# Token rows for the expert blocks: two gathers of whole rows and a way through memory to quarter rows, in place of eight gathers of quarter rows

## The chip, the cores and the metric

The kernel runs on one core of a Trainium2 chip. A core has a matrix engine (TensorE, PE in the profile), a vector engine (VectorE, DVE), a scalar engine (ScalarE, ACT), GpSimd (POOL) and SyncE (SP). On this kernel SyncE does nothing but start plain transfers, and GpSimd starts all transfers whose addresses come from a list (gathers and scatters). The metric is the device time of one execution in microseconds (us); it is shown as the median of several runs, and one more execution is taken with a profiler.

## The reference

Attention over pooled keys and values, then a mixture of experts in which each token goes to one expert. Tokens whose local gate is at or above one half take over the expert of the token before.

```python
k_p = k.reshape(B, H, Sp, 8, D).mean(axis=3); v_p = v.reshape(B, H, Sp, 8, D).mean(axis=3)
scores = scale * np.matmul(q, k_p.transpose(0, 1, 3, 2))
attn_out = softmax(scores) @ v_p                       # B=8, H=8, S=576, D=64
x = attn_out.transpose(0, 2, 1, 3).reshape(B, S, 512)  # 4608 tokens of 512 numbers
logits = np.einsum('bsd,de->bse', x, w_gate)           # 8 experts
for b in range(B):
    prev_e = -1
    for s in range(S):
        fresh_e = int(np.argmax(logits[b, s]))
        e = fresh_e if s == 0 or local_gate[b, s] < 0.5 else (prev_e if prev_e >= 0 else fresh_e)
        prev_e = e
        p = softmax(logits[b, s])
        h = np.maximum(x[b, s] @ w1[e], 0.0)           # 512 -> 1024
        out[b, s] = p[e] * (h @ w2[e])                 # 1024 -> 512
```

## The kernel before, in words

**Two stages.** The first 230 us or so are attention: units of 128 queries, in an order written out by hand (`PLAN`). Each unit's token rows are written to a table in memory, `x_rows`, one row of 512 numbers for each token. For each token a router ranks it within its expert and scatters the token's number and its gate value into lists in memory (`ids`). The second stage, from about 250 us to the end, is the experts: blocks of 256 tokens of one expert each. The first of them stand in hand-written lists (`PLAN_B`, `PLAN_C`; one word is one step, `M1` and `M2` being the two products of block 0), then come `block 1` and a chain of blocks 2, 3, ... under branches (`blocks`), until the tokens run out.

**One block.** Weights are held as a high and a low part, so each product is three products. `l1_two` makes eight groups of hidden columns; `l1_mms` writes group f to one of the buffers `hp` (three of them in block 1, six later), and `l1_h` (ACT copy L338, DVE add L339) and `l1_l` (L343, L344) take it out. `l2(1)` and `l2(0)` (L352) make the two halves of the output rows, `emit_scale` (DVE, L1061) scales a half into `ob`, and `emit_rows` (POOL, L1064) scatters its 128 rows to `out`. Where a block has 128 tokens or fewer, `single` is used in place of `l1_two`.

**How a block's tokens get in.** `ids_load(b+4)` (SP, four transfers into `idp`, L300) reads a piece of the lists. `ids_sum` (DVE, L304, L305) turns it into row numbers of quarter rows, `idk`; `meta` (L308 to L311) picks the token numbers `mi` and gate values `ms` that the output needs. `gather` (POOL, L315) then starts eight gathers, each of 128 quarter rows (512 bytes each), into `xk`, whose partition 32a+s holds quarter a of the tokens s, 32+s, 64+s and so on. With this layout one DVE instruction in `x_turn` (L319) transposes all 32x32 pieces at once, and `x_split` (L324, L325) makes the two parts that TensorE reads. `ahead(b)` does lists, `meta` and `gather` for block b+3, after `l1_two(b)`; the rows are transposed in `x_turn` at the start of block b+2. So `xk` has two buffers. For blocks 2 and 3 these steps are the words `f1` to `f4` of `PLAN_B`, and `x_turn(2)` stands in front of `l1_two(1)`.

**What sets the order.** Each engine runs its own instructions in program order. Two transfers that write the same tensor are ordered by the framework: the second is started when the first has landed. The two scatters of a block both write `out`, so they follow each other in this way. The weights of the next expert are loaded by SP (L207, L211) into `raw1` and `raw2` and split by ACT and DVE (L214, L215, L219, L220) when the expert changes.

Of the kernel before, what the change touches and what calls it, by code (L numbers as in the profile page):

```python
# [16 lines left out]
P = 128  # L17
B, H, S, HD = 8, 8, 576, 64
POOL = 8
# [77 lines left out]
M1:0 M1:1 M1:2 M1:3 i2:0 M1:4 M1:5 f0:0 f1:0 i3:0 f2:0 M1:6 M1:7 YR:0 M2:0 M2:1 M2:2 M2:3 Y1:0 M2:4 M2:5 Y0:0 f3:0 i4:0 f4:0 M2:6 M2:7  # L97
""")
PLAN_C = plan("""
ld:0 M2:8 M2:9 M2:10 M2:11 e1:0 M2:12 M2:13 M2:14 M2:15  # L100
# [3 lines left out]
def moe_attention(ctx: ExitStack, tc: tile.TileContext, q, q_st, k, v, w_gate, w_local, w1, w2, out):  # L104
# [60 lines left out]
    picked = const.tile([P, 2, 2, 5], F32, name="picked")  # L165
    nc.vector.memset(picked, 0.0)
    nc.vector.tensor_scalar(out=picked[:, :, 0, 4], in0=quad.broadcast_to([P, 2]), scalar1=-0.25, scalar2=None, op0=ALU.mult)
# [76 lines left out]
    idp = route.tile([P, 5, TB, 2], F32, name="idp", bufs=1)  # L244
    ids4 = route.tile([P, TB, 2], F32, name="ids4", bufs=1)
    idk = [route.tile([P, TB], I32, name=f"idk{i}", bufs=1) for i in range(2)]
    nc.gpsimd.memset(idp[:, 4], 0.0)
    nc.gpsimd.tensor_copy(out=idp[:, 4, :, 0], in_=quad.broadcast_to([P, TB]))
    x_pc = x_rows.rearrange("n (a d) -> (n a) d", d=PC)
# [53 lines left out]
    def ids_sum(b):  # L303
        nc.vector.tensor_reduce(out=ids4, in_=idp.rearrange("p u j w -> p j w u"), axis=AX.X, op=ALU.add)  # L304
        nc.vector.tensor_copy(out=idk[b % 2], in_=ids4[:, :, 0])  # L305

    def meta(b):
        nc.vector.tensor_tensor(out=picked.rearrange("p h w j -> p h j w")[:, :, 0:4, :],  # L308
# [4 lines left out]
    def gather(b):  # L313
        for j in range(TB):
            nc.gpsimd.indirect_dma_start(out=xk[b % 2][:, j, :], out_offset=None, in_=x_pc,  # L315
                                         in_offset=bass.IndirectOffsetOnAxis(ap=idk[b % 2][:, j:j + 1], axis=0))
# [39 lines left out]
    with ExitStack() as actx:  # L356
# [399 lines left out]
        xk, xtb, xr_t, sp = {}, {}, None, None  # L756
        xgs, xts, xtp = {}, {}, {}

        def do(name, n):
# [144 lines left out]
            elif op == "f1":  # L904
                ids_sum(2)
                meta(2)
            elif op == "f2":
                xk.update({i: ld.tile([P, TB, PC], F32, name="kt", bufs=2) for i in range(2)})
                xr_t = ld.tile([P, KD, 2 * P], F32, name="qt", bufs=4)
                gather(2)  # L910
            elif op == "f3":
                ids_sum(3)
                meta(3)
            elif op == "f4":
                gather(3)
            elif op == "i4":
# [186 lines left out]
    def ahead(b):  # L1103
        ids_sum(b + 3)
        meta(b + 3)
        gather(b + 3)
        ids_load(bass.ds(entry(b + 4, 1, (EN.SP,), NU32 - TB), TB))
# [12 lines left out]
    def rest(b, two):  # L1120
# [10 lines left out]
        emit_rows(b, 1)  # L1131
        l2(0)
# [64 lines left out]
```

## Time and profile before

| what | value |
|---|---|
| median of 3 runs | 695.61 us (692.05 to 696.6) |
| the profiled execution | 693.06 us, span 691.4 us from its first to its last instruction |
| PE busy over the span | 621.9 us (90%) |
| DVE, ACT, POOL busy | 448.8, 272.4, 381.9 us |
| the eight gathers a block (L315) | 176 instructions, 180.7 us busy on POOL, mean 1027 ns |
| moved by transfers started on POOL | 22.60 MB, 10.3% of 16 engines' span |
| moved by transfers started on SP | 74.38 MB, 32.1% |

Busy shares are averages over both stages. An engine's share tells how much it does, not whether anyone waits for it; that is read in a stretch, from the idle time in front of instructions and from what ended it. A time is an instruction's start after the first instruction of the span. A transfer's instruction ends when it has been handed over, not when the data has arrived; the time to landing stands in a view of its own.

### The profile page before, as it was taken

To read this page: it belongs to the slowest core of one execution; us is meant where nothing else is said; L and a number is where in the kernel's file an instruction comes from. 1 tells how busy PE (TensorE), PEld (TensorE's weight loads), DVE (VectorE), ACT (ScalarE), POOL (GpSimd) and SP (SyncE) were. 2 spreads that over 40 slices of the span, in tenths; PEclk is the share of its full clock that TensorE was granted. 3 is DMA by queue.
4 is the path that set the end of the run, shared out by engine and by line. 5 is a ranking of instruction groups with operands and counts; after the bars stand their busy time and mean duration, and the time that the engine had idled before them with its cause. 6 is when DMAs were issued, how large, how long until landed. Compare 5 with 4: busy or idle time off the path is not lost. (4 is left out here: it accounts for less than half of the span.)

```text
span 691.4 us, 11897 instructions
## 1 busy us (share of the span) xinstructions
PE 621.9 (90%) x3588; PEld 526.4 (76%) x3588; DVE 448.8 (65%) x1026; ACT 272.4 (39%) x612; POOL 381.9 (55%) x431
## 2 busy tenths in 40 slices
PE   2878799789698899999999999999999999999990
PEld 1767688678577788878888878788887887888880
DVE  5567589997966764636548647678945478854440
ACT  1134345355454333313326326366613267432230
POOL 5256566876757455565454455474655535555432
PEclk7579799997779899999999999999999999999996
DMA  7988784645431212821114521718722118722111
GB/s 207 298 284 277 258 265 141 195 145 170 128 131 63 77 34 75 297 73 48 55 56 138 192 69 41 294 52 283 271 81 65 42 55 288 274 67 65 40 48 35
DMA packets 50230, 98.10 MB, mean 142 GB/s; under 512 B 23630, under 2 KB 23634, under 8 KB 50132
## 3 DMA queue, kind: packets, MB, share of 16 engines
q1 hardware_dynamic: 39348, 74.38, 32.1%
q0 software_dynamic: 10784, 22.60, 10.3%
q8 instruction: 39, 0.64, 0.4%
q14 instruction: 59, 0.48, 0.2%
HBM read 76.84 MB, written 22.21 MB: 143 GB/s over the span
## 5 line engine op out<-in xcount | busy, mean ns | idle before, releaser
L315 POOL DMA_INDIRECT kt<-x_rows,idk x176 | 180.7, 1027 | 113.8 <-DVE picked L308 64.7
L331 PE MATMUL hp<-x,w1h 128*128 128x512 f32 x376 | 135.9, 402 | 0.1
L352 PE MATMUL o_ps<-w2h,ht_h 128*128 128x512 f32 x312 | 122.8, 394 | 1.5 <-PEq L1128 0.9
L352 PE MATMUL o_ps<-w2h,ht_l 128*128 128x512 f32 x312 | 122.0, 391 | 0.0
L352 PE MATMUL o_ps<-w2l,ht_h 128*128 128x512 f32 x312 | 121.6, 390 | 0.0
L333 PE MATMUL hp<-x,w1l 128*128 128x256 f32 x376 | 106.2, 282 | 0.0
L338 ACT COPY hs<-hp 128x256 f32<-128x256 f32 x94 | 34.8, 370 | 147.4 <-PE hp L333 146.9
L331 PEld LDWEIGHTS hp<-x,w1h 128*128 128x128 f32 x376 | 71.3, 190 | 17.9 <-DVE hs L339 0.6
L567 PE MATMUL op<-vaug,aT 128*128 128x148 f32 (+4 forms) x448 | 77.9, 340 | 2.1 <-ACT aT L377 1.8
L567 PEld LDWEIGHTS op<-vaug,aT 128*128 128x128 f32 (+1 forms) x448 | 69.4, 202 | 8.8 <-ACT aT L377 3.1
L333 PEld LDWEIGHTS hp<-x,w1l 128*128 128x128 f32 x376 | 71.7, 191 | 0.9 <-DVE w1l L215 0.3
L352 PEld LDWEIGHTS o_ps<-w2h,ht_h 128*128 128x128 f32 x312 | 58.6, 188 | 14.6 <-ACT ht_h L961 2.5
L352 PEld LDWEIGHTS o_ps<-w2h,ht_l 128*128 128x128 f32 x312 | 58.5, 188 | 13.5 <-DVE ht_l L962 0.7
L343 ACT ACTIVATE ht_h<-hs 128x256 fp32r<-128x256 f32 x136 | 57.2, 421 | 29.1 <-DVE hs L339 29.1
L352 PEld LDWEIGHTS o_ps<-w2l,ht_h 128*128 128x128 f32 x312 | 58.6, 188 | 11.5
L344 DVE SCALAR_TENSOR_TENSOR ht_l<-hs,ht_h 128x256 fp32r<-128x256 f32 x136 | 59.1, 435 | 5.9 <-ACT ht_h L343 5.6
L339 DVE TENSOR_TENSOR hs<-hp,hs 128x256 f32<-128x256 f32 x94 | 38.7, 415 | 31.3 <-ACT hs L338 30.8
L1061 DVE TENSOR_SCALAR ob<-o_ps,ms 128x512 f32<-128x512 f32 x22 | 16.5, 748 | 51.7 <-PE o_ps L352 50.3
L1064 POOL DMA_INDIRECT out<-ob,mi x22 | 23.0, 1047 | 46.1 <-DVE mi L311 10.8
L383 POOL TENSOR_TENSOR t<-vt_in 128x512 f32<-128x512 f32 (+1 forms) x22 | 25.1, 1140 | 39.1 <-DMA vt_in<-in_v 38.7
L703 POOL DMA_INDIRECT ids<-pm,pos x36 | 35.7, 991 | 19.3 <-DVE pos L700 9.4
L377 ACT COPY osb<-op 128x444 f32<-128x444 f32 (+2 forms) x56 | 26.5, 476 | 47.8 <-PE op L567 43.2
(250 smaller groups left out, 1135.9 us busy)
## 6 DMA issues: line engine op xcount, KB each, us to landing
raw<-in_moe_w SPq DMA_DIRECT2D x56, 512.0 KB
kk<-in_k SPq DMA_DIRECT2D x16, 576.0 KB
vt_in<-in_v SPq DMA_DIRECT2D x16, 512.0 KB
qt<-in_q SPq DMA_DIRECT2D x16, 512.0 KB
x_rows<-xs SPq DMA_DIRECT2D x16, 512.0 KB
kt<-x_rows,idk POOLq DMA_INDIRECT x176, 2.6
vt_in<-in_v SPq DMA_DIRECT2D x8, 256.0 KB
vt_in<-in_moe_w SPq DMA_DIRECT2D x4, 512.0 KB
```

The costliest lines, as they stand in the source:

```text
L315: nc.gpsimd.indirect_dma_start(out=xk[b % 2][:, j, :], out_offset=None, in_=x_pc, in_offset=bass.IndirectOffsetOnAxis(ap=idk[b % 2][:, j:j ...
L331: nc.tensor.matmul(out=ps, lhsT=W1[0][:, kk, f * P:(f + 1) * P], rhs=xt[:, kk].rearrange("p i n -> p (i n)"), start=(kk == 0), stop=False, ...
L333: nc.tensor.matmul(out=ps[:, 0:2 * P], lhsT=W1[1][:, kk, f * P:(f + 1) * P], rhs=xt[:, kk, 0, :], start=False, stop=(kk == KD - 1), skip_g ...
L338: nc.scalar.copy(out=hb[:, 0, :], in_=ps[:, 2 * P:])
L339: nc.vector.tensor_tensor(out=hb[:, 1, :], in0=ps[:, 0:2 * P], in1=hb[:, 0, :], op=ALU.add)
L343: nc.scalar.activation(out=ht[0][:, f, :], in_=hb, func=AF.Relu)
L344: nc.vector.scalar_tensor_tensor(out=ht[1][:, f, :], in0=hb, scalar=0.0, in1=ht[0][:, f, :].bitcast(F32), op0=ALU.max, op1=ALU.subtract)
L352: nc.tensor.matmul(out=to[h], lhsT=ht[i][:, kk, h * P:(h + 1) * P], rhs=W2[j][:, kk, :], start=(n == 0), stop=(n == 3 * KF - 1))
L377: nc.scalar.copy(out=out, in_=in_)
L383: nc.gpsimd.tensor_tensor(out=t4[:n, 0:m], in0=src[:, :, 0:256], in1=src[:, :, 256:512], op=ALU.add)
L567: nc.tensor.matmul(out=out, lhsT=lhs, rhs=rhs if len(out.shape) == 3 else rhs.rearrange("p s x -> p (s x)"), start=all(x[0] != n for x in ...
L703: nc.gpsimd.indirect_dma_start(out=ids[u % 4].rearrange("t m w -> (t m) w"), out_offset=bass.IndirectOffsetOnAxis(ap=pos[:, u:u + 1], axis=0),
```

## The change

The eight gathers of quarter rows become two gathers of 128 whole rows each (2 KB a row) into `xg`, with the token numbers `mi` as row numbers. A new function `quarters` brings them into the layout that `xk` had: SP writes the 256 rows to a scratch table `xd` in memory (two of them, in turn), and then reads them back with four transfers, one for each quarter a, into partitions 32a to 32a+31. `quarters(b+3)` stands in `rest`, after the first scatter of block b and in front of `l2(0)`; for blocks 2 and 3 it stands in the plans as `qr:2` (after `f4`) and `qr:3` (in front of `ld`, the first load of `raw1` and `raw2`). `ids_sum` goes: `idk` and its cast are no longer needed, and the fifth column of `idp`, which added the number of the quarter, goes with it. `xg` uses two buffers of the pool where attention kept keys (`kk`).

```diff
--- before.py
+++ after.py
@@ -94,10 +94,10 @@
 XR:1 L1:4 rR:3 ct:0 rV:3 rP:3 h0:4 h1:4 s:0 s:0 s:0 s:0 s:0 s:0 s:0 s:0 s:0 L1:5 tc:0 cn:0 i1:0 h0:5 h1:5
 tb:0 tb:1 L1:6 h0:6 h1:6 tb:2 tb:3 L1:7 h0:7 h1:7 tb:4 tb:5 tb:6 tb:7 L2:0 L2:1 L2:2 X1:1 L2:3 X1c:1 L2:4
 X0:1 L2:5 X0c:1 L2:6 L2:7 es:1 L2:8 L2:9 so:1 L2:10 L2:11 g1:0 L2:12 L2:13 L2:14 L2:15 es:0 so:0
-M1:0 M1:1 M1:2 M1:3 i2:0 M1:4 M1:5 f0:0 f1:0 i3:0 f2:0 M1:6 M1:7 YR:0 M2:0 M2:1 M2:2 M2:3 Y1:0 M2:4 M2:5 Y0:0 f3:0 i4:0 f4:0 M2:6 M2:7
+M1:0 M1:1 M1:2 M1:3 i2:0 M1:4 M1:5 f0:0 f1:0 i3:0 f2:0 M1:6 M1:7 YR:0 M2:0 M2:1 M2:2 M2:3 Y1:0 M2:4 M2:5 Y0:0 f3:0 i4:0 f4:0 qr:2 M2:6 M2:7
 """)
 PLAN_C = plan("""
-ld:0 M2:8 M2:9 M2:10 M2:11 e1:0 M2:12 M2:13 M2:14 M2:15
+qr:3 ld:0 M2:8 M2:9 M2:10 M2:11 e1:0 M2:12 M2:13 M2:14 M2:15
 """)
 
 @with_exitstack
@@ -162,9 +162,7 @@
     nc.vector.tensor_scalar(out=prow_i, in0=prow_i, scalar1=5, scalar2=None, op0=ALU.arith_shift_right)
     nc.vector.tensor_copy(out=quad, in_=prow_i)
     pickm = const.tile([P, 2, 4, 2], F32, name="pickm")
-    picked = const.tile([P, 2, 2, 5], F32, name="picked")
-    nc.vector.memset(picked, 0.0)
-    nc.vector.tensor_scalar(out=picked[:, :, 0, 4], in0=quad.broadcast_to([P, 2]), scalar1=-0.25, scalar2=None, op0=ALU.mult)
+    picked = const.tile([P, 2, 2, 4], F32, name="picked")
     for j in range(4):
         for w, f in ((0, 0.25), (1, 1.0)):
             nc.vector.tensor_scalar(out=pickm[:, :, j, w], in0=quad.broadcast_to([P, 2]), scalar1=float(j), scalar2=f,
@@ -241,12 +239,9 @@
     ps_r = ctx.enter_context(tc.tile_pool(name="ps_r", bufs=1, space=PSUM))
     ms = [route.tile([P, 2, 2], F32, name=f"ms{i}", bufs=1) for i in range(NM)]
     mi = [route.tile([P, 2], I32, name=f"mi{i}", bufs=1) for i in range(NM)]
-    idp = route.tile([P, 5, TB, 2], F32, name="idp", bufs=1)
+    idp = route.tile([P, 4, TB, 2], F32, name="idp", bufs=1)
     ids4 = route.tile([P, TB, 2], F32, name="ids4", bufs=1)
-    idk = [route.tile([P, TB], I32, name=f"idk{i}", bufs=1) for i in range(2)]
-    nc.gpsimd.memset(idp[:, 4], 0.0)
-    nc.gpsimd.tensor_copy(out=idp[:, 4, :, 0], in_=quad.broadcast_to([P, TB]))
-    x_pc = x_rows.rearrange("n (a d) -> (n a) d", d=PC)
+    xd = [dram.tile([2 * P, D], F32, name=f"xd{i}") for i in range(2)]
 
     idns = [route.tile([P, 4, 2, 2], F32, name=f"idn{i}", bufs=1) for i in range(NS + 1)]
     idms = [route.tile([P, 2, 2], F32, name=f"idm{i}", bufs=1) for i in range(NS + 1)]
@@ -300,20 +295,22 @@
             nc.sync.dma_start(idp[:, u].rearrange("p j w -> p (j w)"),
                               ids[u][:, r, :].rearrange("t j w -> t (j w)").unsqueeze(0).broadcast_to([4, 32, 2 * TB]))
 
-    def ids_sum(b):
+    def meta(b):
         nc.vector.tensor_reduce(out=ids4, in_=idp.rearrange("p u j w -> p j w u"), axis=AX.X, op=ALU.add)
-        nc.vector.tensor_copy(out=idk[b % 2], in_=ids4[:, :, 0])
-
-    def meta(b):
-        nc.vector.tensor_tensor(out=picked.rearrange("p h w j -> p h j w")[:, :, 0:4, :],
+        nc.vector.tensor_tensor(out=picked.rearrange("p h w j -> p h j w"),
                                 in0=ids4.rearrange("p (h j) w -> p h j w", h=2), in1=pickm, op=ALU.mult)
         nc.vector.tensor_reduce(out=ms[b % NM], in_=picked, axis=AX.X, op=ALU.add)
         nc.vector.tensor_copy(out=mi[b % NM], in_=ms[b % NM][:, :, 0])
 
     def gather(b):
-        for j in range(TB):
-            nc.gpsimd.indirect_dma_start(out=xk[b % 2][:, j, :], out_offset=None, in_=x_pc,
-                                         in_offset=bass.IndirectOffsetOnAxis(ap=idk[b % 2][:, j:j + 1], axis=0))
+        for h in range(2):
+            nc.gpsimd.indirect_dma_start(out=xg[b % 2][:, h, :], out_offset=None, in_=x_rows[0:NT + 1],
+                                         in_offset=bass.IndirectOffsetOnAxis(ap=mi[b % NM][:, h:h + 1], axis=0))
+
+    def quarters(b):
+        nc.sync.dma_start(xd[b % 2].rearrange("(h p) d -> p h d", h=2), xg[b % 2])
+        for a in range(4):
+            nc.sync.dma_start(xk[b % 2][32 * a:32 * a + 32], xd[b % 2][:, PC * a:PC * (a + 1)].rearrange("(j s) c -> s j c", s=32))
 
     def x_turn(b):
         nc.vector.transpose(out=xr_t.rearrange("p k (j t) -> p j k t", t=32),
@@ -753,7 +750,7 @@
         first1, first2, lgs = {}, {}, {}
         reg = {}
 
-        xk, xtb, xr_t, sp = {}, {}, None, None
+        xk, xg, xtb, xr_t, sp = {}, {}, {}, None, None
         xgs, xts, xtp = {}, {}, {}
 
         def do(name, n):
@@ -902,17 +899,19 @@
             elif op == "f0":
                 rows_meta(1, NS)
             elif op == "f1":
-                ids_sum(2)
                 meta(2)
             elif op == "f2":
                 xk.update({i: ld.tile([P, TB, PC], F32, name="kt", bufs=2) for i in range(2)})
+                xg.update({i: ld.tile([P, 2 * G * POOL], F32, name="kk", bufs=3)[:, 0:2 * D].rearrange("p (h d) -> p h d", h=2)
+                           for i in range(2)})
                 xr_t = ld.tile([P, KD, 2 * P], F32, name="qt", bufs=4)
                 gather(2)
             elif op == "f3":
-                ids_sum(3)
                 meta(3)
             elif op == "f4":
                 gather(3)
+            elif op == "qr":
+                quarters(n)
             elif op == "i4":
                 ids_load(bass.ds(entry(4, 1, (EN.SP,), NU32 - TB), TB))
             elif op == "i3":
@@ -1101,7 +1100,6 @@
         load2(rl2, nx)
 
     def ahead(b):
-        ids_sum(b + 3)
         meta(b + 3)
         gather(b + 3)
         ids_load(bass.ds(entry(b + 4, 1, (EN.SP,), NU32 - TB), TB))
@@ -1129,6 +1127,7 @@
                 l2(1)
         emit_scale(b, 1)
         emit_rows(b, 1)
+        quarters(b + 3)
         l2(0)
         with tc.If(chg > 0):
             weights2(nx)
```

**SyncE at the start of block 1.** The queue between the last list load (`i4`, the last of four `idp` transfers) and the first weight loads (`raw`). Before:

```order
L300 DMA idp<-ids_67 128x1x16 [waits DMAHW1_49]
L225 TENSOR_LOAD tab
L207 ISA
L207 DMA raw_3020<-in_moe_w 128x1024 [waits DMASW1_49,DMASW2_49,DMASW0_49,DMASW3_49,PE_49,Activation_49]
L207 ISA
L207 DMA raw_3020<-in_moe_w 128x1024
```

In the changed kernel (`kk` is the pool's name for `xg`, `kt` that for `xk`):

```order
L295 DMA idp<-ids_67 128x1x16 [waits DMAHW1_49]
L311 DMA xd_188<-kk 128x2x512 [waits DMASW5_49,DMASW4_49]
L313 DMA kt<-xd_188 32x8x128 [waits DMAHW6_49,Activation_49]
L313 DMA kt<-xd_188 32x8x128 x2
L313 DMA kt<-xd_188 32x8x128 [waits DMAHW2_49]
L311 DMA xd_189<-kk 128x2x512 [waits DMAHW3_49,DMASW7_49,DMASW6_49]
L313 DMA kt<-xd_189 32x8x128 [waits DMAHW4_49,DMAHW3_49,Activation_49]
L313 DMA kt<-xd_189 32x8x128 [waits DMAHW5_49]
L313 DMA kt<-xd_189 32x8x128
L313 DMA kt<-xd_189 32x8x128 [waits DMAHW7_49]
L223 TENSOR_LOAD tab
```

Ten transfers now stand between the list load and the first weight load: for block 2 and then for block 3 one write to `xd`, and four reads behind it that wait for that write.

**GpSimd in a block of the chain, from its gathers to its last scatter.** The words are the same in every block. Before:

```order
L315 DMA kt<-x_rows,idk_191 128x128 x8
L225 TENSOR_LOAD tab
L1123 COMPARE_AND_BRANCH
L1123 UNCONDITIONAL_BRANCH x2
L1128 UNCONDITIONAL_BRANCH
L1064 DMA out<-ob_2465,mi_184 4608x512
L1133 COMPARE_AND_BRANCH
L1133 UNCONDITIONAL_BRANCH x2
L1064 DMA out<-ob_2465,mi_184 4608x512
```

In the changed kernel:

```order
L307 DMA kk<-x_rows,mi_180 128x512 x2
L223 TENSOR_LOAD tab
L1121 COMPARE_AND_BRANCH
L1121 UNCONDITIONAL_BRANCH x2
L1126 UNCONDITIONAL_BRANCH
L1063 DMA out<-vt_in,mi_183 4608x512
L1132 COMPARE_AND_BRANCH
L1132 UNCONDITIONAL_BRANCH x2
L1063 DMA out<-vt_in,mi_183 4608x512
```

Two instructions stand in front of the two scatters where there were eight.

## Rows read from the trace of the kernel before

**Rows 1.** The head of the profile's page: the span, each engine's busy time with its share and its instructions, and the span in 40 slices of 17.3 us (busy tenths of PE and POOL, and the clock that TensorE was granted in tenths of 2.4 GHz).

```profile
span 691.4 us, 11897 instructions
...
PE 621.9 (90%) x3588; PEld 526.4 (76%) x3588; DVE 448.8 (65%) x1026; ACT 272.4 (39%) x612; POOL 381.9 (55%) x431
...
PE   2878799789698899999999999999999999999990
...
POOL 5256566876757455565454455474655535555432
PEclk7579799997779899999999999999999999999996
```

**Rows 2.** Busy time by stretch of the span. Columns: stretch and its length, then for each engine busy us and instructions, then granted clock, share of the DMA engines, GB/s.

```profile
276.00:300.00 24.00, 24.00 (x121) 20.29 (x120) 11.83 (x28) 6.64 (x18) 13.85 (x15) 1.00 0.65 231
300.00:400.00 100.00, 99.39 (x498) 83.60 (x497) 57.47 (x123) 37.94 (x86) 50.56 (x51) 1.00 0.29 95
400.00:500.00 100.00, 98.25 (x488) 81.84 (x487) 76.00 (x134) 53.35 (x98) 58.05 (x53) 1.00 0.49 169
500.00:600.00 100.00, 98.55 (x485) 81.74 (x485) 65.74 (x126) 44.86 (x91) 53.02 (x50) 1.00 0.41 141
600.00:675.00 75.00, 75.00 (x374) 63.29 (x374) 36.12 (x90) 20.94 (x57) 36.19 (x38) 1.00 0.18 54
675.00:691.00 16.00, 0.54 (x3) 0.11 (x1) 0.75 (x1) 0.00 (x0) 3.61 (x4) 0.68 0.11 36
```

**Rows 3.** POOL in order of time from the end of one block to the end of the span: start, duration, engine, line, operation; in brackets the idle time in front and what ended it.

```profile
654.95 1.02 POOL L1064 DMA_INDIRECT out<-vt_in,mi  x1 [0.30 <-issue]
658.53 1.14 POOL L1064 DMA_INDIRECT out<-vt_in,mi  x1 [2.56 <-DVE hs L339]
667.15 0.98 POOL L315 DMA_INDIRECT kt<-x_rows,idk  x1 [7.48 <-DVE picked L308]
668.43 0.96 POOL L315 DMA_INDIRECT kt<-x_rows,idk  x1 [0.30 <-issue]
...
675.94 0.94 POOL L315 DMA_INDIRECT kt<-x_rows,idk  x1 [0.30 <-issue]
677.19 1.02 POOL L1064 DMA_INDIRECT out<-ob,mi  x1 [0.30 <-issue]
681.62 1.01 POOL L1064 DMA_INDIRECT out<-ob,mi  x1 [3.40 <-issue]
```

**Rows 4.** DVE in order of time in the last block, with the same columns.

```profile
667.21 0.17 DVE L311 CAST mi<-ms 128x2 int32<-128x2 f32 x1
670.13 0.75 DVE L1061 TENSOR_SCALAR ob<-o_ps,ms 128x512 f32<-128x512 f32 x1 [2.76 <-PE o_ps L352]
675.57 0.75 DVE L1061 TENSOR_SCALAR ob<-o_ps,ms 128x512 f32<-128x512 f32 x1 [4.69 <-PE o_ps L352]
```

**Rows 5.** SP in order of time at the start of block 1 (the last three list loads; the first four weight loads).

```profile
271.69 2.02 SPq L300 DMA_DIRECT2D idp<-ids  x3
274.94 1.98 SPq L207 DMA_DIRECT2D raw<-in_moe_w  x4
```

**Rows 6.** DVE in order of time from the scaling of block 0's last half to the first add of block 1.

```profile
276.19 0.75 DVE L1061 TENSOR_SCALAR ob<-o_ps,ms 128x512 f32<-128x512 f32 x1 [3.96 <-PE o_ps L352]
276.86 1.23 DVE L319 STREAM_TRANSPOSE qt<-kt 128x1024 f32<-128x1024 f32 x1
278.05 0.42 DVE L339 TENSOR_TENSOR hs<-hp,hs 128x256 f32<-128x256 f32 x1
```

**Rows 7.** PE in order of time: the first product of block 1, and the first one of its fourth group of hidden columns, which uses the buffer of the first group again.

```profile
275.99 0.39 PE L331 MATMUL hp<-x,w1h 128*128 128x512 f32 x1
280.22 0.40 PE L331 MATMUL hp<-x,w1h 128*128 128x512 f32 x1
```

**Rows 8.** SP: the start of a write of 512 KB of token rows to memory (4 KB pieces).

```profile
228.68 0.32 SPq L614 DMA_DIRECT2D x_rows<-xs  x1
```

**Rows 9.** GB/s of all transfers from 228 to 236 us in 40 slices of 0.2 us: the write of rows 8 and behind it, in the last slices that are not zero, two smaller ones.

```profile
GB/s 307 348 185 41 0 0 0 266 369 451 389 410 389 369 215 297 154 318 266 41 0 0 0 0 0 0 0 0 0 0 0 0 0 0 0 0 0 0 0 0
```

**Rows 10.** The small plain loads `idn`: durations (ns, minimum, median, maximum) and start of the first and of the last.

```profile
L259 SPq DMA_DIRECT2D idn<-ids x12: 537/538/637, 166.0 to 252.8; - x12
```

**Rows 11.** DVE: the instruction that waited for the last of these loads.

```profile
254.87 0.18 DVE L263 TENSOR_REDUCE idm<-idn 128x4 f32<-128x16 f32 x1 [2.76 <-DMA idn<-ids]
```

**Rows 12.** Transfers started on POOL, with the median us from start to landing: gathers of 128 whole rows (2 KB each), gathers of 128 quarter rows, and scatters of 128 whole rows.

```profile
qt<-x_rows,idr POOLq DMA_INDIRECT x2, 3.7
kt<-x_rows,idk POOLq DMA_INDIRECT x176, 2.6
out<-vt_in,mi POOLq DMA_INDIRECT x20, 2.8
out<-ob,mi POOLq DMA_INDIRECT x22, 4.3
```

**Rows 13.** POOL: one of the gathers of 128 whole rows.

```profile
257.31 0.96 POOL L273 DMA_INDIRECT qt<-x_rows,idr  x1 [0.30 <-issue]
```

**Rows 14.** DVE in order of time: the lists of block 4 (L304), and the `x_turn` instructions of blocks 3 and 4 (L319).

```profile
289.19 0.28 DVE L304 TENSOR_REDUCE ids<-idp 128x16 f32<-128x80 f32 x1
299.70 1.25 DVE L319 STREAM_TRANSPOSE qt<-kt 128x1024 f32<-128x1024 f32 x1 [0.53 <-DMA kt<-x_rows,idk]
312.12 1.25 DVE L319 STREAM_TRANSPOSE qt<-kt 128x1024 f32<-128x1024 f32 x1
```

**Rows 15.** The first part of the weight splits, all of them: durations (ns), and the start of the first and of the last.

```profile
L214 ACT CAST w1h<-raw x24: 1040/1047/1054, 369.1 to 584.0; 128x1024 fp32r<-128x1024 f32 x24
```

**Rows 16.** Busy time by stretch, with the columns of rows 2: the weight loads at the start of block 1.

```profile
275.00:287.00 12.00, 12.00 (x69) 10.35 (x68) 7.74 (x17) 5.53 (x15) 7.57 (x8) 1.00 0.95 339
```

**Rows 17.** Busy time by stretch, with the columns of rows 2, in the last part of attention.

```profile
200.00:223.00 23.00, 20.73 (x179) 18.21 (x178) 16.16 (x47) 12.56 (x28) 16.70 (x15) 1.00 0.13 47
223.00:230.00 7.00, 3.01 (x18) 1.80 (x18) 6.34 (x13) 1.62 (x6) 5.81 (x6) 1.00 0.35 106
230.00:237.00 7.00, 7.00 (x30) 6.15 (x31) 5.00 (x20) 3.04 (x9) 0.00 (x0) 0.51 0.25 81
```

**Rows 18.** PE: the instruction that ended the long idle time inside the second of these stretches.

```profile
229.93 0.46 PE L646 MATMUL tp<-ident,ab 128*2 128x128 f32 x2 [2.62 <-DVE erow L651]
```

## The prediction

> **What bounds the kernel now.** I read the page's head first, then busy time by stretch, then the two places in order of time where the chain of blocks begins and ends. The 40 slices show TensorE at nine tenths or more, at full clock, from slice 14 to the last but one [rows 1]. The stretches say it more sharply: from 276 to 675 us TensorE is busy 395.2 of 399 us, and GpSimd some 212 [rows 2]. So in the chain of blocks nothing that GpSimd does is waited for by TensorE, and at most 3.8 us could be won there by anything that doesn't shorten products. The gathers, at 180.7 us the costliest group of the page, lie beside products.
>
> GpSimd is on the path in one place, the end. TensorE has nothing left after 675.6 us [rows 2, 4], but the span goes on to 691.4. In the last block the eight gathers, for a block that will not run, occupy GpSimd from 667.15 to 676.88. The first scatter starts behind them at 677.19, though its data were ready at 670.13 + 0.75 = 670.88. The second starts at 681.62, though its data were ready at 675.57 + 0.75 = 676.32: it waits until the first has landed [rows 3, 4]. After it come its landing and the closing of the program, 691.4 - 681.6 = 9.8 us.
>
> **The change part by part.**
>
> *The end.* Two gathers replace eight. A gather of whole rows costs POOL the same as one of quarter rows, 0.96 us against 0.94 to 0.98 [rows 3, 13]. It now waits for `mi`, two steps later than before; without the cast of `idk` that is some 0.1 to 0.2 us. So the two gathers run from about 667.3 to 669.6, the first scatter at its data (670.9), and it has landed 3.6 us later (the distance at which the second follows it in the block before, 654.95 to 658.53 [rows 3]), at 674.5. The second then starts at its own data, 676.3, plus a reaction of 0.1 to 0.2: 676.5 in place of 681.6. **Gain 5.1 us.** What is late next is the work that SP now has for the block that won't run: second gather at 668.6, landing 3.7 later [rows 12], write 2.8, reads 3.9 (both below), so 679.0, against the landing of the second scatter at 676.5 + 2.8 = 679.3 [rows 12]. They meet; if the dead transfers land later, they take the gain back one for one.
>
> One rule would deny this term. The Trainium skill, "DMA: Bandwidth & Descriptors", section "Issuing engines are not separate DMA queues", says that spreading starts over engines saves only the time that starting takes, usually small beside the transfer. By that the end would gain next to nothing. Here a start takes 0.94 us and comes every 1.25 us, and eight of them in a row stand in front of a scatter [rows 3], so I go by the rows.
>
> *The chain of blocks.* Removed from GpSimd: six starts a block, 6 x 1.25 = 7.5 us, all under products. Removed from DVE: a cast of 0.17 us a block. Added to SP: five transfers a block, one of which waits for a gather and four for a write; what is queued behind them on SP is the load of `raw2` and the next list load, which waits for DVE in the next block anyway. The new way in must be done before `x_turn`. The tightest place is block 1 to block 3: lists at 289.19, `x_turn(4)` at 312.12, so 22.9 us [rows 14]. The new chain needs 0.9 for the four DVE steps, 1.3 to the second gather, 3.7 to its landing, 2.8 for the write and 3.9 for the reads: 12.6 us. Where weights are being loaded, up to 2 MB go ahead of it in the same queue, some 6 us at 339 GB/s [rows 16]. Cover remains: 0 us. If it were gone, every block would pay the overrun, since DVE stands still in `x_turn` and the adds behind it free TensorE's buffers. The weights themselves come later: the first load of `raw1` and `raw2` moves behind `qr:2` and `qr:3`, by about 10 us, but its first use is at 369.1 [rows 15]. 0 us.
>
> *The start of block 1.* Here the cover is missing. `x_turn(2)` ran at 276.86, directly after the scaling of block 0's last half at 276.19 [rows 6]. Now `qr:2` stands behind the list load `i4` on SP, whose last transfer is handed over at 271.69 + 2.02 = 273.71 [rows 5]; the gathers of block 2, from 263.5 on, are long in by then. Neither a copy to `xd` nor a read back from it is in this trace, so both are bounded by neighbours:
>
> - Write of 512 KB: a like one started at 228.68, and at 370 to 450 GB/s its bytes are through at about 230.8 [rows 8, 9], that is 2.1 us; to landing at least 2.2. Upwards, a 256 KB scatter lands in 2.8 [rows 12], and 256 KB more at 339 GB/s add 0.8: 3.6. I take 2.8, nearer to the like write, because pieces are 2 KB here and the gathers of block 3 run beside it.
> - Four reads: their starts come 0.5 to 0.7 apart (four weight loads in 1.98, three list loads in 2.02 [rows 5]), so 1.8 to the last. It lands 2.1 later, as the small loads do (254.87 - 252.8 [rows 10, 11]); upwards 4.3 as the slower scatters [rows 12]. I take 3.9 for the four, between 3.6 and 6.5.
>
> So `x_turn(2)` can start at 273.7 + 2.8 + 3.9 = 280.4, between 279.5 and 283.8. Behind it on DVE stands the add of the first hidden group, which ended 1.6 us after `x_turn` began (276.86 to 278.47 [rows 6]) and frees a buffer that TensorE wants again at 280.22 [rows 7]. TensorE therefore stands for 280.4 + 1.6 - 280.2 = **1.8 us**, between 0.9 and 5.2. After that the buffers cycle as before.
>
> The Trainium skill, "DMA: Bandwidth & Descriptors", section "Anatomy of one DMA — SWDGE (gpsimd) path", fits about 2.0 us fixed for each transfer plus its bytes over 436 GB/s; by that, as an estimate, the write would take 3.2 and the last read 2.3 from its start, and the stand would be 2.4 us. No row here shows that fit for transfers that SP starts.
>
> *The sum.* 693.06 - 5.1 + 1.8 + 0.1 = 689.9 for an execution like the profiled one. That one lies 2.55 below the median of 695.61, so on the median: 695.61 - 3.2 = **692.4 us**. The runs shown spread over 4.5 us, and for this kernel a difference below about 1% (7 us) can hardly be told from none.
>
> **The rivals.**
>
> 1. *The clock answers the stand* (0.25). In the last part of attention TensorE was busy 3.0 of 7 us, with one gap of 2.62, and in the next 7 us the granted clock was 0.51; in the 23 us before, busy 20.7 of 23, it stayed at 1.00 [rows 17, 18]. A stand of 1.8 us inside otherwise full work is like neither of them. If the clock falls to 1.2 GHz for as long as it did there, half of 7 us is lost: -3.2 + 3.4 gives 695.8. The Trainium skill, "TensorE: Matmul & The Clock Gate", Part 1, says that the gate follows how busy the array has recently been, which is the direction of these rows.
> 2. *Slower: `qr:2` takes longer than the end gives back* (0.12). Place: SP at 273.7 to `x_turn(2)`. Against the gain of 5.1 it decides from a stand of 5.1, that is `x_turn(2)` at 283.8 or 10.1 us for write and reads in place of 6.7. For it: the reads are of 512-byte pieces, of which there is no row for a plain load, and each waits out a round trip to memory. Against: the like write and small loads above. At 12 us the stand is 7.1, and such a stand takes the clock with it: 695.6 - 5.1 + 7.1 + 1.7 = 699.3.
> 3. *The change doesn't shorten the end* (0.08): the dead block's transfers, or the closing of SP behind them, land some 3 us after the scatter. A scatter's landing of 4.3 in place of 2.8 [rows 12] shows that 1.5 us happens. Gain 2.1 in place of 5.1: 695.4. With no gain at all, because starting transfers is not what the end waits for, it would be 697.4; this is what the rule of the Trainium skill in the part on the end ("DMA: Bandwidth & Descriptors") comes to.
> 4. *No stand at all* (0.10): the write lands in 2.2 and the reads in 3.6, as in the lowest rows, and TensorE stands 0.9 or less: 690.5 to 691.5.
> 5. *Late in every block* (0.04): the way in takes over 22.9 us in most blocks, 20 blocks at 1 us or more: 712 or above.
>
> My forecast has the remaining 0.41.
>
> **How the numbers follow.** The forecast's own range is 689 to 694.5. Rivals 1 and 3 end at 695.4 to 697.4, rival 2 mostly below 700. The range 688.8 to 698.5 leaves out rival 5, the worse half of rival 2 and lucky runs. Faster by over 1% means below 688.7: the whole gain at the end, no stand, and a median from the low side of the spread, 0.06. Slower by over 1% means above 702.6: rival 5 and the far end of rival 2, 0.06. Within 1%: 0.88.
>
> **What the profile after would show.** Right: two gathers a block of about 1 us each; products filling the chain of blocks as before; the second scatter of the last block starting within 0.5 us of its scaling, and some 10 us from there to the end; DVE idle in front of `x_turn(2)` for about 3 us, put down to a read from `xd`; TensorE idle once, near 280 us, for 1 to 3 us. Wrong: idle time in front of `x_turn` in later blocks; the span ending on SP's transfers; the clock below 1.00 near 285 us; or attention, which the change hardly touches, moving by itself.

## The result and the profile after

The changed kernel is slower, by a little: 698.27 us (median of 12 runs, 696.35 to 700.43) against 695.21 us for the kernel before beside it (12 runs), a ratio of 1.0051, 95% interval 1.0028 to 1.0074. (A median is of all runs; a ratio leaves out runs more than 1.5% above the fastest of their kernel, and it isn't the quotient of the two medians.) I had forecast 692.4, which is 3.2 us less than before, and the direction is wrong. The range of 688.8 to 698.5 takes the time in, but only the rivals had stretched it so far; the forecast's own range ended at 694.5. The profiled execution took 697.89 us, its span is 696.2 us.

The page's head of the changed kernel (the view of [rows 1]):

```profile
span 696.2 us, 11821 instructions
...
PE 624.8 (90%) x3588; PEld 528.6 (76%) x3588; DVE 448.9 (64%) x1002; ACT 272.3 (39%) x612; POOL 248.7 (36%) x297
...
PE   2888898788688899799999999999999999899993
```

GpSimd lost 133 us of work and TensorE gained nothing from it. TensorE's row has a seven (278.5 to 295.9 us) and an eight (591.8 to 609.2 us) inside the chain of blocks, where before it had nines. Behind them are two stands (times in which TensorE waits), one foreseen too small and one not foreseen.

**The start of block 1.** SP, POOL, DVE and PE of the changed kernel in order of time (the views of [rows 5 to 7]), then busy time by stretch (columns of rows 2):

```profile
275.26 0.42 SPq L311 DMA_DIRECT2D xd<-kk  x1
279.94 1.81 SPq L313 DMA_DIRECT2D kt<-xd  x4
```

```profile
273.21 0.94 POOL L307 DMA_INDIRECT kk<-x_rows,mi  x1 [5.34 <-DVE mi L303]
274.45 0.95 POOL L307 DMA_INDIRECT kk<-x_rows,mi  x1 [0.30 <-issue]
275.70 1.02 POOL L1063 DMA_INDIRECT out<-ob,mi  x1 [0.30 <-issue]
```

```profile
284.57 1.25 DVE L316 STREAM_TRANSPOSE qt<-kt 128x1024 f32<-128x1024 f32 x1 [6.16 <-DMA kt<-xd]
```

```profile
286.18 0.80 PE L328 MATMUL hp<-x,w1h 128*128 128x512 f32 x1 [4.33 <-DVE hs L336]
```

```profile
282.00:286.00 4.00, 0.00 (x0) 0.00 (x0) 1.43 (x2) 0.00 (x0) 0.30 (x1) 0.99 0.93 267
286.00:289.40 3.40, 3.22 (x10) 2.74 (x11) 1.64 (x5) 1.23 (x4) 0.00 (x0) 0.51 0.61 152
```

The write is handed over at 275.26 and the reads, which wait for it, at 279.94: 4.7 us. `x_turn(2)` starts 4.6 us after that. DVE stands 6.16 us in front of it, TensorE 4.33, and for the next 3.4 us TensorE runs at 1.2 GHz (granted clock 0.51), which costs half of them, 1.7 us.

**An expert change, a single block, an expert change, at 575 to 605 us.** SP, ACT, DVE and PE in order of time:

```profile
575.37 2.15 SPq L205 DMA_DIRECT2D raw<-in_moe_w  x4
579.97 0.39 SPq L311 DMA_DIRECT2D xd<-kk  x1
586.84 1.87 SPq L313 DMA_DIRECT2D kt<-xd  x4
589.04 2.08 SPq L209 DMA_DIRECT2D raw<-in_moe_w  x4
```

```profile
599.90 1.05 ACT L217 CAST w2h<-raw 128x1024 fp32r<-128x1024 f32 x1 [1.03 <-DMA raw<-in_moe_w]
```

```profile
600.99 1.23 DVE L218 TENSOR_TENSOR w2l<-raw,w2h 128x1024 fp32r<-128x1024 f32 x1 [0.86 <-ACT w2h L217]
...
602.79 1.24 DVE L316 STREAM_TRANSPOSE qt<-kt 128x1024 f32<-128x1024 f32 x1
```

```profile
604.39 0.50 PE L328 MATMUL hp<-x,w1h 128*128 128x512 f32 x1 [2.41 <-DVE hs L336]
```

SP hands over the four loads of `raw1`, then the write of block b + 3. That one lands behind 2 MB of weights, so SP stands until 586.84 for the reads, and `raw2` is issued only at 589.04. The next change of expert, one short block later, wants `raw2` split by 602. ACT waits for its four pieces one after another, for the last until 599.9, so the splits hold DVE until 602.2, `x_turn` comes behind them and TensorE stands 2.41 us. In the kernel before, no wait of TensorE there is longer than 0.6 us.

**The end.** DVE, POOL and SP of the last block (the views of [rows 3, 4]), then the closing of the program by line (ns minimum, median, maximum; start of the first and of the last), of the changed kernel (L1192) and of the kernel before (L1193):

```profile
685.16 0.75 DVE L1060 TENSOR_SCALAR ob<-o_ps,ms 128x512 f32<-128x512 f32 x1 [4.69 <-PE o_ps L349]
```

```profile
677.14 0.98 POOL L307 DMA_INDIRECT kk<-x_rows,mi  x1 [12.17 <-DVE mi L303]
678.43 0.97 POOL L307 DMA_INDIRECT kk<-x_rows,mi  x1 [0.30 <-issue]
680.75 1.02 POOL L1063 DMA_INDIRECT out<-ob,mi  x1 [1.36 <-DVEq L1132]
686.19 1.01 POOL L1063 DMA_INDIRECT out<-ob,mi  x1 [4.42 <-POOLq L1147]
```

```profile
683.54 0.39 SPq L311 DMA_DIRECT2D xd<-kk  x1
686.39 1.89 SPq L313 DMA_DIRECT2D kt<-xd  x4
```

```profile
L1147 SPq EVENT_SEMAPHORE  x9: 17/17/17, 692.0 to 692.6; - x9
L1192 SPq EVENT_SEMAPHORE  x14: 17/28/28, 694.2 to 696.1; - x14
L1192 POOLq DRAIN  x3: 46/107/2112, 691.4 to 695.9; - x3
```

```profile
L1193 POOLq DRAIN  x3: 46/107/4232, 686.3 to 691.1; - x3
```

Both scatters start within 0.3 us of their data. From the last scaling to the end of the span it is 696.2 - 685.2 = 11.0 us, where it was 691.4 - 675.6 = 15.8 [rows 1, 4]: 4.8 won. But another engine now ends last. GpSimd's long closing instruction, 4.2 us before and 2.1 now, ends at 691.4 + 2.1 = 693.5. SP passes its waits for the quarters of the dead block (one behind the last, which doesn't exist) at 692.0 to 692.6, and its own closing waits run from 694.2. That SP's quarters set the end is shown by e5 below.

The spans differ by 4.8 us: 4.3 + 1.7 + 2.4 - 4.8 = +3.6, and 1.6 more from attention, whose long wait ends at 231.5 in place of 229.9 [rows 18]; that is 0.4 too many. Such an offset comes and goes (in e9 and e10 below that wait ends at 231.7 in the kernel before and at 230.9 in the changed one). So the 3.6 are to be compared with 3.1 by the medians and 3.5 by the ratio.

### The profile page after: what moved, and what is told of

The parts are those of the page before. It is cut to its first block, busy times and chain, and to the rows that moved or that the text cites. A ratio compares the mean times of both kernels' runs of the same rounds, so it can differ in the third digit from the quotient of the medians.

```text
span 696.2 us, 11821 instructions
## 1 busy us (share of the span) xinstructions
PE 624.8 (90%) x3588; PEld 528.6 (76%) x3588; DVE 448.9 (64%) x1002; ACT 272.3 (39%) x612; POOL 248.7 (36%) x297
## 5 line engine op out<-in xcount | busy, mean ns | idle before, releaser
L307 POOL DMA_INDIRECT kk<-x_rows,mi x44 | 44.3, 1008 | 190.5 <-DVE mi L303 183.8
L1063 POOL DMA_INDIRECT out<-ob,mi x22 | 25.0, 1136 | 74.8 <-DVE ob L1060 27.4
L1063 POOL DMA_INDIRECT out<-vt_in,mi x20 | 23.0, 1151 | 68.3 <-DVE vt_in L1060 27.6
```

The costliest lines, as they stand in the source:

```text
L307: nc.gpsimd.indirect_dma_start(out=xg[b % 2][:, h, :], out_offset=None, in_=x_rows[0:NT + 1], in_offset=bass.IndirectOffsetOnAxis(ap=mi[b ...
L1063: nc.gpsimd.indirect_dma_start(out=outv, out_offset=bass.IndirectOffsetOnAxis(ap=mi[b % NM][:, h:h + 1], axis=0), in_=ob[b % 2][:, h, :], ...
```

## Experiments

My theory after the result: three effects add, two stands from the order on SP and a gain at the end. The rivals are in the expectations. e1 to e4 ran together on one chip, e5 to e8 on another, e9 to e11 on a third.

**e1**, one word moved in the order written by hand:

```diff
-... Y0:0 f3:0 i4:0 f4:0 qr:2 M2:6 M2:7
+... Y0:0 f3:0 qr:2 i4:0 f4:0 M2:6 M2:7
```

> The changed kernel with one step moved in the hand-written order at the end of the routing: the transfers of block 2 (`qr:2`) stand in front of the loads of the list for block 4 (`i4:0`) on SP, not behind them. The rows of block 2 have landed at about 270.9 us in the changed kernel's trace, its write starts only at 275.3.
> Theory (the stand of 4.3 us at the start of block 1 and the 3.4 us at half clock behind it, 1.7 us lost, come from the place of `qr:2` in SP's order alone): the write starts at about 271, `x_turn(2)` is ready between 277.7 (write 2.8, reads 3.9) and 280.0 (4.6 and 4.4), TensorE doesn't stand and the clock stays up. 698.3 less 6.0 is 692.3, a ratio of 0.996 to the kernel before.
> Rival A (the stand comes from DMA traffic that the change adds, not from the order): block 1 starts about as late, the ratio stays at 1.003 to 1.005.
> Rival B (the stand goes, the clock falls there all the same): 698.3 less 4.3 is 694.0, a ratio of 0.998.

Measured: 696.37 us, ratio 1.0006 (0.9984 to 1.0029); one run of the twelve took 1091.5 us, which nothing here explains. SP, DVE and PE, and two stretches:

```profile
273.38 0.41 SPq L311 DMA_DIRECT2D xd<-kk  x1
276.29 1.81 SPq L313 DMA_DIRECT2D kt<-xd  x4
```

```profile
284.05 1.25 DVE L316 STREAM_TRANSPOSE qt<-kt 128x1024 f32<-128x1024 f32 x1 [3.33 <-DMA kt<-xd]
```

```profile
285.66 0.49 PE L328 MATMUL hp<-x,w1h 128*128 128x512 f32 x1 [1.50 <-DVE hs L336]
...
601.89 0.50 PE L328 MATMUL hp<-x,w1h 128*128 128x512 f32 x1 [1.84 <-DVE hs L336]
```

```profile
280.00:290.00 10.00, 8.50 (x49) 7.18 (x48) 5.90 (x12) 3.67 (x10) 1.00 (x1) 1.00 0.72 203
...
603.00:607.00 4.00, 4.00 (x15) 3.37 (x14) 3.79 (x10) 3.46 (x11) 0.15 (x1) 0.57 0.94 313
```

Half right, and short of the 6.0 us. The write, with nothing beside it now, takes 2.9 us, and the clock stays up. But the reads, which took 4.6 us in the changed kernel, take 7.8: the gathers of block 3 run beside them (POOL 275.5 to 277.7 in this trace) where they ran beside the write before. A stand of 1.5 us is left. Rival A had a share, though its ratio of 1.003 lies outside the interval: traffic counts as well as order. The stand at 602 us stays (1.84), and here the clock falls behind it, which in the first trace of the changed kernel it did not.

**e2**, in `rest`:

```diff
-    quarters(b + 3)
     l2(0)
     with tc.If(chg > 0):
         weights2(nx)
+    quarters(b + 3)
```

> The changed kernel with the transfers of each expert block placed behind the loads of `raw2` in `rest`, so that at a change of expert SP issues raw1, raw2 and then the write and the reads of the quarters.
> Theory (the 2.4 us that TensorE stands at 602 us, at a change, a single block and a change in a row, come from `raw2`, which SP held for about 10 us behind the reads of the quarters): `raw2` is issued within 3 us of `raw1`, that stand goes, the one at the start of block 1 stays. 698.3 less 2.4 is 695.9, a ratio of 1.001 to the kernel before.
> Rival A (with 4 MB instead of 2 in front of it the write takes longer still, the quarters are late instead): a stand in front of `x_turn` at the same place of up to 3 us, ratio 1.005 or above.
> Rival B (the stand at 602 us has nothing to do with the order on SP): it stays at 2.4 us, ratio 1.005.

Measured: 697.07 us, ratio 1.0024 (1.0001 to 1.0047). SP:

```profile
573.13 2.17 SPq L205 DMA_DIRECT2D raw<-in_moe_w  x4
578.10 4.87 SPq L209 DMA_DIRECT2D raw<-in_moe_w  x4
584.34 0.39 SPq L311 DMA_DIRECT2D xd<-kk  x1
589.66 1.86 SPq L313 DMA_DIRECT2D kt<-xd  x4
```

`raw2` is issued 2.8 us after `raw1` has been handed over, and TensorE has no idle time over 0.6 us at 600 us; the start of block 1 is unchanged (a stand of 4.42). By the trace the theory holds; the time alone wouldn't show it, since its interval overlaps that of the changed kernel. The reads of the quarters start 2.8 us later (5 us later against the products of the single block, which come 2.3 us earlier in this trace), and nobody waits for them. The gain is below 2.4 us because the end grew from 11.0 to 12.8 us, from the last scaling (680.6) to the end of the span (693.4).

**e3**, the kernel before with one line changed, so that from block 4 on six of the eight gathers are left out:

```diff
-        for j in range(TB):
+        for j in range(TB if b < 4 else 2):
```

> The kernel before, with two of the eight gathers of quarter rows left out of nothing but the count: from block 4 on only the first two of the eight are issued (the other six quarters are not fetched). No transfer through memory is added, SP's order is that of before.
> Theory (the end of the program is shorter because GpSimd has two gathers in front of the second scatter, and not eight): from TensorE's last matmul to the end of the span about 15.8 us before, 11.1 in the changed kernel; here 11.1 or less. Of the 11.1 the transfers of a block that doesn't exist take a part, since SP ends its last wait for them at 692.0 and the program's end follows from SP: without them 9.5 us. No stand at 280 or 602 us. So 695.2 less 4.7 to 6.3 is 690.5 to 688.9, a ratio of 0.991 to 0.993.
> Rival (the gain at the end has another cause than the count of gathers): 15.8 us as before, ratio 1.000.

Measured: 690.65 us, ratio 0.9926 (0.9902 to 0.9949). DVE and POOL at the end, and GpSimd's closing:

```profile
680.31 0.75 DVE L1061 TENSOR_SCALAR ob<-o_ps,ms 128x512 f32<-128x512 f32 x1 [4.69 <-PE o_ps L352]
```

```profile
681.34 1.01 POOL L1064 DMA_INDIRECT out<-ob,mi  x1 [4.42 <-POOLq L1148]
```

```profile
L1193 POOLq DRAIN  x3: 46/107/3081, 686.2 to 689.8; - x3
```

The span ends at 690.1, 9.8 us after the scaling. Fewer gathers are worth 6 us at the end by the trace and 5.2 by the ratio, if nothing is put in their place. Of the 6, 5.0 are the first term of my sum: the second scatter starts 0.3 us after its data (680.31 + 0.75) and not 5.3. The other 1.0 is the closing behind it, 8.8 us in place of 9.8; GpSimd's long closing instruction takes 3.1 in place of 4.2.

**e4**, both moves, of e1 and e2:

> The changed kernel with both moves: `qr:2` in front of `i4:0`, and the transfers of each block behind the loads of `raw2`.
> Theory (three sums that add: the stand and the clock at the start 6.0 us, the stand at 602 us 2.4 us, and the gain at the end of 4.7 us, which stays): 698.3 less 8.4 is 689.9, a ratio of 0.992 to the kernel before, faster than both kernels.
> Rival (another cost of the change, spread over the blocks, that these two stalls only hide): the ratio stays above 0.996.

Measured: 693.45 us, ratio 0.9967 (0.9946 to 0.9987): faster than both kernels, but 3.5 us above the sum. Stretches (columns of rows 2), and GpSimd's and SP's closing:

```profile
276.00:300.00 24.00, 22.99 (x116) 19.22 (x116) 10.69 (x25) 6.67 (x18) 3.96 (x4) 1.00 0.89 297
580.00:606.00 26.00, 25.17 (x126) 20.64 (x127) 22.07 (x41) 15.79 (x30) 7.33 (x6) 1.00 0.82 284
```

```profile
L1192 SPq EVENT_SEMAPHORE  x14: 17/28/28, 686.7 to 690.3; - x14
L1192 POOLq DRAIN  x3: 46/107/2112, 682.8 to 690.1; - x3
```

A stand of 1.0 us is left at the start (reads of 7.1 us), and the end is 13.2 us long (677.2 to 690.4). GpSimd is through with its long closing instruction at 684.9, SP's waits go on to 690.3. The ratio lies above 0.996, as the rival had it, but no cost is spread over the blocks: from 276 to 580 us TensorE is idle 3.9 us, 1.0 of them in that stand, and 3.5 in the kernel before. So the rival's cause falls, and what is missing from the sum lies in the stand and in the end. Why the end of e2 and e4 is about 2 us longer than in the changed kernel is not shown: the dead block's reads start 1.0 us behind the last scaling there (678.17 in e4) and 1.2 in the changed kernel.

**e5**, e4 and in `rest`:

```diff
-    quarters(b + 3)
+    with tc.If(live > b + 3):
+        quarters(b + 3)
```

where `live` is the count of blocks, read by SP once; 19 writes to `xd` are left of 22.

> The kernel of e4 (both moves) in which SP issues the transfers of block b + 3 only where that block exists (a branch on the count of blocks).
> Theory (in the changed kernel, in e2 and in e4 the end of the program follows from SP, which waits for quarters that nobody uses; in e4 their reads land at 684.8, GpSimd's own last drain ends at 684.9, SP's last one at 689.3): without them GpSimd is last again. From TensorE's last matmul to the end of the span 13.3 us in e4, here 9 to 10; 3.5 us less, a ratio of 0.992 to the kernel before, against 0.997 in e4.
> Rival (SP's end is long for another reason, its code after the last block): 13 us as in e4, ratio 0.997.

Measured: 690.90 us. On this chip the kernel before took 741.6 us, and nowhere else; no profile shows why. (Its granted clock there, 0.906 to 0.933, doesn't tell it: on the other chips runs of 692.5 to 697.3 us had 0.926 to 0.931.) So for e5 to e8 the times themselves are compared, not ratios, and across chips. From the last scaling (679.00) to the end of the span (687.3) it is 8.3 us, 4.9 less than e4, so the rival falls. A stand of 1.2 us is left at the start (reads of 7.5). GpSimd again ends last, its long closing instruction running from 684.0 to 686.1:

```profile
L1197 SPq EVENT_SEMAPHORE  x14: 17/28/28, 683.5 to 687.2; - x14
L1197 POOLq DRAIN  x3: 46/107/2112, 684.0 to 687.0; - x3
```

**e6** and **e7** ask which company makes the reads of block 2 long. e6 is e4 with the list loads behind the transfers of block 3, e7 is e4 with the gathers of block 3 behind both scatters of block 0:

```diff
-... Y0:0 f3:0 qr:2 i4:0 f4:0 M2:6 M2:7
-qr:3 ld:0 M2:8 ...
+... Y0:0 f3:0 qr:2 f4:0 M2:6 M2:7
+qr:3 i4:0 ld:0 M2:8 ...
```

```diff
-... Y0:0 f3:0 qr:2 i4:0 f4:0 M2:6 M2:7
-qr:3 ld:0 M2:8 ...
+... Y0:0 f3:0 qr:2 i4:0 M2:6 M2:7
+M2:8 ...
 x_turn(2)
+run(plan("f4:0 qr:3 ld:0"))
```

> The kernel of e4 with the four loads of the list for block 4 (`i4:0`) moved once more, behind the transfers of block 3 (`qr:3`). In e4 the reads of block 2 take 7.0 us (273.2 to 280.2), 2.8 us after DVE has become free for `x_turn(2)`; beside them run the gathers of block 3, a scatter and these list loads.
> Theory L (the many small packets of the list loads make the reads long): the reads take 4 to 4.5 us, `x_turn(2)` starts when DVE is free, TensorE doesn't stand; 1.0 us less than e4, ratio 0.995.
> Theory G (the gathers of block 3 make them long): the reads still take 6 us or more, the stand of about 1 us stays, ratio as in e4.

> The kernel of e4 with the gathers of block 3 (`f4:0`) behind both scatters of block 0 on GpSimd, with the transfers of block 3 and the first loads of raw weights behind them on SP; the list loads stay between the reads of block 2 and these.
> Theory G (the gathers of block 3 make the reads of block 2 long): the reads take 4 to 4.5 us in place of 7.0, `x_turn(2)` starts when DVE is free, TensorE doesn't stand; ratio 0.995 against 0.997 in e4.
> Theory L (the list loads do): the reads still take 6 us or more, the stand of about 1 us stays, ratio as in e4.
> The raw weights start some 5 us later than in e4; their first use is at about 369, so that costs nothing by either.

Measured: e6 696.22 us (6 runs, 694.54 to 701.71), e7 693.83 us (6 runs, 689.63 to 698.00), e4 693.45 us on the other chip: the times don't show the 1 us that either theory promised, and the traces have to decide. In e6 the reads start at 276.96 and `x_turn(2)` at 284.44, 7.5 us, and TensorE stands 1.44. In e7, on DVE and SP:

```profile
276.49 1.85 SPq L313 DMA_DIRECT2D kt<-xd  x4
```

```profile
281.54 1.25 DVE L316 STREAM_TRANSPOSE qt<-kt 128x1024 f32<-128x1024 f32 x1 [0.76 <-DMA kt<-xd]
```

5.05 us, and no stand. Theory G holds in its cause, with 5 us where it said 4 to 4.5, and theory L falls: beside the gathers of block 3 the reads take 7.1 to 7.8 us (e1, e4, e5, e6), without them 4.6 (after, e2, e10) to 5.1 (e7, e8, e11). e7 also moves the write of block 3 away from these reads, but that write is not the cause: in the changed kernel it is handed over at 281.86, while the reads of block 2 are under way, and they take 4.6. The write of block 2 takes 4.7 to 5.1 (after, e2, e10) against 2.9 with nothing beside it; beside it there are these gathers, a scatter and the last list loads, and no run separates them.

**e8 and e11**, everything: e5, with the step order of e7 and `i4:0` behind `qr:3`.

> Everything together: the kernel of e5 (both moves, no transfers for blocks that don't exist) with the gathers and transfers of block 3, the list for block 4 and the first raw weights behind the scatters of block 0.
> Theory (the changed kernel keeps its whole gain at the end once nothing that it adds is waited for): no stand at the start of block 1 and at 602 us, 9 to 10 us from the last matmul to the end; 695.9 less 6 to 7 us is 689 to 690, a ratio of 0.990 to 0.991, the fastest of these kernels.
> Rival (what moves behind is late at its next place: the lists for block 4 or the quarters of block 3): a stand of 1 us or more between 290 and 320 us, ratio 0.993 or above.

> The kernel of e8 once more, for a ratio to the kernel before on an ordinary chip: 688.9 us against 695.5 is 0.990, the interval below 0.993. Rival (its gain in e8 belonged to that chip): 0.995 or more.

Measured: e8 688.94 us; e11, on a third chip, 689.90 us, ratio 0.9917 (0.9886 to 0.9949). The expected 0.990 lies inside the interval, whose upper end is above the 0.993 that I had set for it; the rival's 0.995 lies outside. Stretches of e8:

```profile
276.00:300.00 24.00, 24.00 (x121) 20.29 (x120) 10.83 (x25) 6.64 (x18) 5.86 (x6) 1.00 0.52 166
...
580.00:606.00 26.00, 25.05 (x125) 20.30 (x125) 22.56 (x42) 16.24 (x31) 9.96 (x6) 1.00 0.82 276
```

Both stands are gone (no wait of TensorE from 276 to 322 us or from 574 to 612 us is over 0.6 us, so the rival falls too), and the end takes 8.4 us. By the medians it is the fastest of these kernels.

**e9 and e10**, both kernels once more:

> The kernel before once more, unchanged, with a profile. Beside e5 to e8 it took 741.6 us (11 runs, 737 to 748), 46 us more than in every other measurement, while the changed kernel's descendants e5 to e8 took 689 to 696 there, as they should.
> Theory (it depends on the chip and concerns the eight gathers of quarter rows): on a chip as in the first measurements 695 us; where it is 741 again, the profile shows TensorE waiting for quarter rows in the block loop (`x_turn` idle on the gathers), and nothing of that in the changed kernel.
> Rival (a slower memory or a lower clock for everything on that chip): then e10 and e11 are slow with it.

> The changed kernel once more, unchanged, for its ratio beside e11: 1.003 to 1.007 where the kernel before takes 695 us. The stand at the start of block 1 (4.3 us, then 3.4 us at half clock) and the one at about 602 us (2.4 us) stand in the profile again, being set by SP's order and not by chance; the rival (one execution's chance) has one of them gone.

Measured: before 695.27 us, its ratio to itself 0.9996; the 741.6 us didn't come again, but this was a third chip, so the theory wasn't tested and the 741.6 us stays unexplained. After 699.35 us, ratio 1.0026 (0.9992 to 1.0060): just below the 1.003 to 1.007 that I had expected, with an interval that takes in 1 and overlaps the first one. So that the changed kernel is slower is clear of noise in the first measurement only. Its two stands came again, as expected, both with the clock down behind them this time:

```profile
285.74 0.80 PE L328 MATMUL hp<-x,w1h 128*128 128x512 f32 x1 [4.66 <-DVE hs L336]
...
604.93 0.50 PE L328 MATMUL hp<-x,w1h 128*128 128x512 f32 x1 [2.02 <-DVE hs L336]
```

```profile
285.00:292.00 7.00, 6.26 (x19) 5.38 (x20) 3.93 (x10) 2.90 (x8) 0.00 (x0) 0.51 0.64 193
...
606.00:610.00 4.00, 4.00 (x15) 3.43 (x14) 3.79 (x10) 3.46 (x11) 0.19 (x1) 0.58 0.85 272
```

Behind the first stand the clock stays at 1.2 GHz from 285.7 to about 292, which costs some 3.1 us and not the 1.7 of the first trace.

## Why the prediction was wrong, step by step

I had forecast 3.2 us less than before, and the medians show 3.1 more. Two steps failed: the price of the write and the reads at the start of block 1, with the clock behind the stand, and the 0 us for the chain of blocks.

- *The end*, gain 5.1: measured 4.8, and that they are so near is in part luck. The step on the second scatter was right: it starts 0.3 us after its data and not 5.3, which is 5.0. The closing behind it takes 10.0 us where I kept 9.8, but it is made of other parts. GpSimd's own became shorter, and SP became last, by the dead block's quarters, of which I had written that they "meet" the scatter's landing. Where they are left out the end takes 8.3 to 8.5 us (e5, e8, e11) and not 11.0, so they cost 2.6 here, and 4.9 in e4. That is the mechanism of rival 3, hidden by a shorter closing that I hadn't foreseen. For the other half of rival 3, no gain at all, I had named the Trainium skill ("DMA: Bandwidth & Descriptors", "Issuing engines are not separate DMA queues"), which calls the time that starting a transfer takes usually small beside the transfer. In this place it isn't: with two starts in place of eight and no other edit the end is 6 us shorter (e3).
- *The start of block 1*, a stand of 1.8: measured 4.33. The mechanism and its place were right, the two terms mis-sized: write 4.7 in place of 2.8, reads 4.6 in place of 3.9. (The write is also handed over 1.55 us later than I had it, at 275.26; but the last scaling of block 0 comes 1.47 later in this trace, so that this hardly counts.) My 2.8 is what the write takes with nothing beside it (2.9 in e1); my 3.9 lies below every length that a trace shows for the reads of block 2 (4.6 to 7.8). I had named the gathers of block 3 as the write's company and yet allowed them 0.6 us at most, and my upper bound for the write, 3.6, was too low. The fit of the Trainium skill ("DMA: Bandwidth & Descriptors", "Anatomy of one DMA — SWDGE (gpsimd) path"), made for transfers that GpSimd starts, gives 3.2 us as an estimate for the write. That is near the 2.9 that it takes alone, and the fit has no term for company.
- *The clock* (rival 1, 0.25): it came. In the first trace it was at half for 3.4 us, which costs 1.7 us and not 3.4; in e10 it cost some 3.1. So rival 1 and the mechanism of rival 2 happened together.
- *The chain of blocks*, 0 us: this is the step that failed without a range. I had written that the load of `raw2` is queued behind the quarters on SP, and then cleared only the first use of the first weights, at 369 us. I never looked for the place where the distance between two changes of expert is shortest. There it cost 2.4 us, and e2 shows that the order on SP did it: with the same transfers behind `raw2` the stand is gone.
- *The sum* misses by 698.3 - 692.4 = 5.9 us. The terms miss by 2.5 and 1.7 at the start, 2.4 at 602 us and 0.3 at the end, 6.9 together. The medians show 6.3, each difference taken against its own median before (695.61 and 695.21). Rival 5 didn't happen: of the 304 us from 276 to 580 TensorE is idle 7.2, 4.3 of them in the first stand, and the rest, 2.9, is no more than the 3.5 in the kernel before. By stretch:

```profile
276.00:580.00 304.00, 296.82 (x1465) 248.56 (x1464) 185.28 (x358) 125.70 (x261) 65.34 (x61) 0.99 0.56 179
```

  Rival 2 had the sign, the mechanism and the place. I let it decide from a stand of 5.1 us; 4.3 were enough, because the clock and the stand at 602 us came on top.

## What to carry to other kernels

Price a new transfer by what will run beside it, not by a row of the same size that ran alone: here company was worth 1.8 to 2.2 us on a write of 512 KB and 2 to 3 us on the four reads behind it. When a queue gets an instruction that waits, list all that stands behind it on that queue, and look for the one place in the program where each of those has the least slack; an average place says nothing. And where the end is shortened on one engine, see what the other engines still have to wait for, work for blocks that don't exist above all.

## What the runs showed of the hardware

- The same four reads of 128 KB from memory took 4.6 to 5.1 us without the two gathers of whole rows beside them and 7.1 to 7.8 with them. The many small list loads beside them made no difference (7.5 us without them in e6, 7.1 with them in e4).
- Whether the clock falls behind a stand isn't told by the stand's length alone: it stayed at 1.00 behind 1.50 us (e1) and 2.41 us (after, at 602 us), and fell behind 1.84 (e1, at 600 us), 2.02 (e10) and 4.33 (after).
- A write of 512 KB took 2.9 us to its landing with nothing beside it (e1, e4 to e8, e11) and 4.7 to 5.1 beside two gathers, a scatter and list loads (after, e2, e10).
- GpSimd's long closing instruction took 4.2 us in the kernel before, 3.1 with two of its eight gathers (e3), and 2.1 where whole rows are gathered; what sets it no run here shows.
